# Windowed attention and a four-expert attention layer on one core: zero products, output buffers and a new list of steps

## The chip, the core and the metric

The kernel runs on one core of a Trainium2 chip. The core has five engines with queues of their own: TensorE (PE; its weight loads are PEld), VectorE (DVE), ScalarE (ACT), GpSimd (POOL) and SyncE (SP), which here only issues DMAs. ACT can issue DMAs too. The metric is the device time of one execution in microseconds, lower is better.

## The reference, cut to what matters

```python
# q, k, v: (8 batches, 8 heads, 576 positions, 64), float32
scores = q @ k^T / 8;  keep |i - j| <= 32;  x = softmax(scores) @ v      # (8, 8, 576, 64)
x = x transposed to (8, 576, 512)
w = weights of the 2 largest of 4 gate logits x @ w_gate, softmax over the two
for e in range(4):                                                       # experts, head size 64
    a = causal softmax((x @ wq[e]) @ (x @ wk[e])^T / 8)
    out += w_e * ((a @ (x @ wv[e])) @ wo[e])                             # (8, 576, 512)
```

## The kernel before

All of it is unrolled. A string, `ORDER`, lists some 900 steps, and a loop at the end of the kernel calls one small function for each; so the list sets the order on every engine's queue, and each queue is worked off in order. A step's name is its function and its indices: the first digit is the batch, the next ones the head group, the half or the pair; what stands behind `:` is the engine or the kind of load (`a` ACT, `v` DVE, `g` POOL; `e` a load on SP's queue, `f` one on ACT's), and behind `@` stand the PSUM banks. PSUM has 8 banks; a step that writes a bank waits until the reader of its last content is done.

First half, for a batch `b` and a group `g` of four heads. `lq`, `lk` load q and k (576 KB; the last digit 1 or 2 marks a half of 288 KB) into three rotating buffers each, `qn0` to `qn2` and `kn0` to `kn2` (`NAT`, chosen by (2b+g) mod 3). `tq`, `tk` turn them on DVE into `Tqn`, `Tkn`. `sc` makes the scores of one half of the positions, 80 small products on PE; `ex` takes their exponential on ACT; `mk` multiplies by the window mask on POOL or DVE. `lv` loads v, `vc` copies parts of it to other rows; `av` is the product with v, `un` divides by the sum (DVE). `xt`, `xf`, `xb` transpose the result and bring it to `XTB`.

Second half. `ga`, `gt`, `ge`, `gm`, `gu` make the gate weights. `pp`, `pe` make the experts' q and k, `pv`, `ve` their v; `ps` the scores, `xe` the exponential (ACT), `se` the causal part (POOL), `po` the product with v, `oe` the scaling (DVE), `pt`, `ot` or `dt` the transposed result, `py` the output product. `ye` copies an output part `w` (0, 1: 256 rows; 2: 64 rows) from PSUM to an SBUF tile that `ysb(b, w)` names, and `st` stores it. Before the change the tile is one of three, `Y0` to `Y2`, with 3b+w counted modulo 3, so part `w` always uses `Yw` and has to wait for its store of the batch before. The same three tiles stage the experts' weights at the start (`lw`, then casts `cw`).

`zz` is four products of 128x512 zeros whose result nobody reads. `s_ones`, `s_zero`, `s_pads` clear tiles on DVE. A load is given one more dependence in code: it follows the last PE instruction that stands ahead of it in the list,

```python
        if last_pe[0] is not None:
            tc.add_manual_dep(r.ins, last_pe[0].ins.name, ...
```

so the place of a load among the PE steps sets its earliest issue, and loads that stand ahead of every PE step start at once.

Of the kernel before, what the change touches and what calls it, by code (L numbers as in the profile page):

```python
# [24 lines left out]
NOE = 4  # L25

ORDER = """
    s_ones lq000:e s_ident s_zero lk000:e zz1@3 lq100:e lq011:f lk012:e lk100:e tq000:e tk000:e zz3@6 lk011:f zz2@6
# [4 lines left out]
    av00@0 un03@4 cw11:a un00@0 xt01@6 lq200:e mk1000:v lv10 xf01:a@6 av01@2 mk1001:g un01@2 lk200:e av04@6 xb01:g
    vc10:a un04@6 mk1011:v xt00@4 xf00:a@4 cw10:a xt02@1 sc110@62 cw01:a ex1100@6 lw3 ex1101@2 xb00:g xf02:v@1 xb02:g
    sc111@04 mk1010:g lv14 mk1101:g pp010@6 lwg lv22 lk210:e tq200:e ex1111@4 vc11:g ex1110@0 lq210:e pe010:a@6
    tk200:e pp001@4 pe001:v@4 cw00:a mk1111:v pp011@2 pe011:a@2 pp000@6 mk1110:v pe000:a@6 sc200@40 av12@2 ex2001@0
    ps012@6 lw2 ex2000@4 un12@2 xe012@6 mk1100:g ps000@0 mk2000:g xe000@0 lv23 av10@4 av11@6 ps03@0 cw3:g ps002@2
    xe03@0 un10@4 se012 un11@6 ps011@4 xe002@2 tq210:e av14@1 xt10@6 lk300:e xe011@4 av13@2 mk2001:g cw2:g se000 lv21
    ps001@4 xe001@4 ga0@0 un13@2 lv20 un14@1 xf10:a@6 xt11@2 xf11:a@2 xt12@1 sc201@64 xb10:g xb11:g lq300:e tk210:e
    lv24 xf12:a@1 ex2011@4 pv00@2 lq400:e xb12:g gt0@0 ex2010@6 ga1@1 ge0@0 vc21:a sc210@46 ve00:a@2 lq310:e tk300:e  # L40
    gt1@1 pp101@2 ge1@1 gm0@0 ex2100@4 gm1@1 gu0@0 mk2011:g gu1@1 vc20:g ex2101@6 lk400:e pe101:a@2 mk2010:g pp100@4
    pe100:a@4 sc211@26 pp111@0 ex2110@2 ps100@2 lk310:e tq300:e lv33 mk2101:g ps101@4 mk2100:g ex2111@6 av21@6
    pe111:v@0 pv11@1 mk2110:g xe100@2 xe101@4 un21@6 ve11:a@1 se001 mk2111:g se011 av20@2 pv01@4 av22@0 ve01:a@4
    av23@4 un20@2 un22@0 lv34 ps102@2 ps010@6 lv30 un23@4 se002 av24@1 un24@1 xt21@4 pp110@0 xe102@2 xe010@6 xf21:a@4
    sc300@26 pe110:v@0 lv42 ex3001@6 ex3000@2 sc301@40 xb21:g xt20@6 ex3010@4 se03 xt22@2 se010 se102 xf20:a@6 tk310:e
    tq310:e lv32 lv31 pv10@4 mk3010:g lv41 po00@6 ex3011@0 xf22:v@2 mk3011:v se101 ve10:a@4 ps13@0 ps111@2 po01@4
    se100 xe13@0 xe111@2 mk3001:g oe00@6 ps110@0 sc311@62 xb20:g xb22:g lk500:e xe110@0 oe01@4 sc310@40 ex3110@6
    lq410:e pp201@6 ex3111@2 lv43 lk410:e tk400:e se13 ex3101@0 tq400:e mk3000:v vc31:g ex3100@4 pp200@0 mk3101:g
    pe201:a@6 pe200:a@0 pp210@2 ps200@4 ps112@6 pp211@0 se110 pe210:v@2 vc30:g mk3100:g xe200@4 sc401@24 xe112@6
    pe211:a@0 ex4010@2 tq410:e po10@6 oe10@6 mk3110:g se112 ex4011@4 lv40 ps210@0 av31@2 mk3111:g ps201@4 xe210@0  # L50
    un31@2 tk410:e vc40:g sc400@60 xe201@4 ex4000@6 ps212@4 xe212@4 ex4001@0 av33@2 av32@6 ps211@4 un33@2 ps23@0
    av34@2 ga2@3 xe211@4 pt01@5 xe23@0 un32@6 lq500:e un34@2 pt00@6 ot00:a@6 se111 pt10@2 ot01:v@5 xt31@4 se23 lq510:e
    ot10:a@2 gt2@3 sc411@60 se200 ge2@3 xf31:a@4 xb31:g se201 se212 pv21@2 av30@4 ex4111@0 mk4011:v ve21:a@2 lq600:e
    gm2@3 ex4110@6 lv44 gu2@3 sc410@20 un30@4 vc41:a mk4000:g tq500:e xt30@4 tk500:e mk4111:g pv20@6 ex4100@2 lv50
    xt32@3 ex4101@0 xf30:a@4 py01@0 xf32:a@3 lk510:e xb30:g ve20:a@6 se210 ps202@2 ye01:v@0 xb32:a po11@4 mk4101:g
    pp301@6 mk4010:g xe202@2 sc500@20 oe11@4 pe301:a@6 sc501@64 ex5000@2 ex5001@0 lk600:e pp310@2 tq510:e mk4110:g
    ex5010@6 pp300@6 py02@0 ex5011@4 av43@4 mk4100:g tk510:e lv54 pe310:v@2 pe300:a@6 lv53 un43@4 mk4001:g lv63 av40@6
    pv31@1 ye02:a@0 ps300@2 lv52 un40@6 ve31:a@1 xe300@2 av41@0 un41@0 av42@4 lv61 ps301@2 ps302@6 ga3@1 se211 xe302@6
    un42@4 gt3@1 lv51 xe301@2 ge3@1 se202 av44@0 lv62 un44@0 mk5011:g gm3@1 xt41@6 gu3@1 py00@2 xf41:a@6 pt11@5 xt42@4
    xb41:g xt40@6 mk5001:g ye00:a@2 tk600:e xf42:a@4 po20@0 se302 se301 pp311@2 xf40:a@6 ot11:a@5 pe311:a@2 oe20@0  # L60
    lq610:e xb40:g pv30@4 ve30:v@4 ps311@2 xb42:g sc511@60 xe311@2 ex5111@0 st01 sc510@42 ex5110@6 mk5000:g lk610:e
    ex5100@4 po21@0 mk5010:g lv60 ga4@6 ps33@4 ex5101@2 vc51:g ps312@2 tq600:e vc50:a xe312@2 oe21@0 xe33@4 mk5100:g
    pv40@0 gt4@6 ge4@6 lk700:e tq610:e py11@2 gm4@6 pt20@7 se300 pp401@4 ve40:a@0 pp410@0 ot20:v@7 ye11:a@2 gu4@6
    vc60:g sc600@26 pe401:a@4 ex6000@2 pe410:v@0 sc601@04 tk610:e mk5110:g ex6010@0 mk5111:g mk5101:g se311 se33
    tk700:e lq700:e pp400@2 po30@0 vc61:g ex6001@6 pe400:a@2 pp411@6 ex6011@4 av51@4 oe30@0 lv64 un51@4 pe411:a@6
    av50@2 av53@0 pv41@6 ve41:a@6 av52@4 ps43@6 un50@2 un53@0 un52@4 ps310@2 ps401@0 xe43@6 av54@6 xt50@4 mk6011:g
    pt21@7 xe310@2 xe401@0 un54@6 sc611@20 ot21:v@7 tq700:e xf50:a@4 sc610@46 ex6110@2 ex6111@0 ps400@2 xt51@0 se312
    ex6100@4 ex6101@6 xe400@2 xb50:g mk6110:v xt52@4 mk6111:v st00 se310 mk6010:v st02 xf52:v@4 py10@6 av62@2 xf51:a@0
    un62@2 se401 py12@5 ye10:a@6 av63@0 ye12:a@5 se43 un63@0 ps402@4 lq710:e ps411@2 xb52:a mk6101:v xe402@4 mk6100:v
    xe411@2 xb51:g pp511@6 se402 pe511:a@6 pp500@0 sc700@42 pe500:a@0 mk6001:v sc701@60 ex7000@4 lv70 ex7001@2 ps410@4  # L70
    ex7010@6 mk7001:g xe410@4 st12 mk6000:v ex7011@0 po31@2 st11 pp501@6 pp510@4 pe501:a@6 av60@6 tq710:e lk710:e
    oe31@2 pe510:v@4 ps53@0 xe53@0 un60@6 st10 lv71 ps502@4 ps501@2 pv51@0 se400 py22@1 xe502@4 dt31 ve51:v@0 xe501@2
    lv73 av61@6 ye22:v@1 dt30 un61@6 ps412@4 py21@0 lv72 xe412@4 po40@6 ye21:v@0 ps500@2 st21 oe40@6 ps512@0 tk710:e
    ga5@5 av64@4 xe512@0 xt61@0 gt5@5 se412 lv74 xe500@2 un64@4 xt60@6 xf61:a@0 py20@2 se411 ye20:a@2 ge5@5 pv50@0
    xf60:v@6 se410 gm5@5 mk7000:g xt62@2 xf62:a@2 xb60:g xb62:a py31@6 ve50:a@0 ye31:a@6 vc71:a po41@2 xb61:g se501
    gu5@5 oe41@2 mk7011:g pp611@4 se502 se500 pp600@0 pe600:v@0 pe611:a@4 pp601@6 pe601:v@6 se53 sc710@02 sc711@64
    ex7100@0 ex7101@2 ex7111@4 mk7100:v po50@0 vc70:g mk7101:g pp610@4 ex7110@6 st20 ps601@6 mk7110:g oe50@0 py30@2
    pe610:v@4 ps602@0 ye30:v@2 xe601@6 mk7010:g ps612@6 dt41 av70@4 xe602@0 st22 av71@2 ps511@0 mk7111:v xe612@6
    un70@4 ps610@6 un71@2 xe511@0 av74@4 xe610@6 un74@4 se602 st31 ga6@5 ps600@2 ps611@0 xe600@2 av73@6 py32@4 xe611@0
    gt6@5 ye32:a@4 un73@6 av72@2 st30 ps63@0 xe63@0 xt70@6 xt72@4 ge6@5 ps510@0 un72@2 xf72:v@4 xt71@2 xf70:a@6 dt40  # L80
    st32 xe510@0 se511 dt50 py41@6 pv60@0 xb72:g se611 se601 xb70:g gm6@5 xf71:a@2 se512 se610 py42@3 ye41:v@6
    ve60:a@0 ye42:v@3 pv61@2 py40@6 gu6@5 se510 se612 ve61:a@2 se600 po51@0 ye40:a@6 xb71:g pp711@2 oe51@0 st42 st41
    pp701@4 se63 pe701:a@4 pp700@0 pe711:v@2 pe700:a@0 dt51 pp710@6 pe710:a@6 po61@2 ps73@4 ps701@6 py51@0 oe61@2 st40
    xe73@4 ps702@4 ps710@2 xe701@6 po60@6 dt61 xe702@4 ye51:a@0 oe60@6 pv70@4 xe710@2 py50@6 se702 ps700@0 ps712@2
    ve70:a@4 xe700@0 dt60 xe712@2 ye50:v@6 ga7@5 pv71@7 gt7@5 py52@4 se700 se73 ye52:v@4 ve71:a@7 ge7@5 se701 gm7@5
    st51 gu7@5 ps711@0 py61@6 st50 po701@4 xe711@0 py60@2 oe701@4 ye61:a@6 st52 se711 se712 st61 ye60:a@2 po711@1
    se710 po700@7 py62@6 pt701@4 st60 oe711@1 oe700@7 ye62:a@6 po710@6 pt711@5 ot701:a@4 ot711:a@5 py711@3 ye711:a@3
# [581 lines left out]
```

## Time and profile before

| | us |
|---|---|
| median of 3 runs (range) | 236.62 (236.04 to 237.95) |
| the profiled execution, whole | 235.26 |
| its span, first to last instruction | 233.5 |
| PE busy in the span | 215.5 |
| mean granted clock of TensorE | 0.971 |

The span is what the trace shows; 1.76 us of the execution lie around it. The profiled execution is 1.36 us shorter than the median.

### The profile page before, as it was taken

To read this page: it belongs to the slowest core of one execution; us is meant where nothing else is said; L and a number is where in the kernel's file an instruction comes from. 1 tells how busy PE (TensorE), PEld (TensorE's weight loads), DVE (VectorE), ACT (ScalarE), POOL (GpSimd) and SP (SyncE) were. 2 spreads that over 40 slices of the span, in tenths; PEclk is the share of its full clock that TensorE was granted. 3 is DMA by queue.
4 is the path that set the end of the run, shared out by engine and by line. 5 is a ranking of instruction groups with operands and counts; after the bars stand their busy time and mean duration, and the time that the engine had idled before them with its cause. 6 is when DMAs were issued, how large, how long until landed. Compare 5 with 4: busy or idle time off the path is not lost.

```text
span 233.5 us, 12313 instructions
## 1 busy us (share of the span) xinstructions
PE 215.5 (92%) x5516; PEld 171.3 (73%) x5516; DVE 179.1 (77%) x366; ACT 156.1 (67%) x232; POOL 137.3 (59%) x173
## 2 busy tenths in 40 slices
...
GB/s 241 409 173 238 167 221 273 239 218 218 298 176 107 146 183 211 11 219 181 186 164 136 253 192 104 140 3 104 158 259 199 177 107 121 55 140 121 225 215 201
DMA packets 60518, 41.97 MB, mean 180 GB/s; under 512 B 50736, under 2 KB 51760, under 8 KB 60464
## 3 DMA queue, kind: packets, MB, share of 16 engines
...
q10 hardware_dynamic: 432, 0.85, 1.0%
...
## 4 chain that ended last, share of the span: by engine, by line
PE 65%; DVE 9%; ACT 2%; issue 2%; DMA 2%; SPq 0%; ACTq 0%; DVEq 0%
PE PS L178 58%; PE PS L181 7%; DVE A L342 2%; DVE Tkn L293 2%; DVE Tqn L293 2%; DMA out_dram<-Y 2%; DVE Y L172 1%; DVE QKE L172 1%; ACT V L170 1%; ACT VE L170 0%; DVE OE L571 0%; ACT A L338 0%; DVE XN L370 0%; ACT OTT L170 0%; ACT AT L511 0%
## 5 line engine op out<-in xcount | busy, mean ns | idle before, releaser
L342 POOL TENSOR_TENSOR A<-A,MASKP 128x576 f32<-128x576 f32 x48 | 68.0, 1432 | 15.3 <-ACT A L338 15.2
L515 ACT ACTIVATE ATE<-PS 128x1024 bf16<-128x1024 f32 x48 | 47.6, 1022 | 14.4 <-PE PS L178 14.2
L338 ACT ACTIVATE A<-PS 128x576 f32<-128x576 f32 x64 | 38.4, 651 | 21.8 <-PE PS L178 21.6
L178 PE MATMUL PS<-Tqn,Tkn 32*64 32x128 f32 (+3 forms) x2560 | 46.5, 283 | 6.4 <-DVE Tkn L293 2.6
L178 PEld LDWEIGHTS PS<-Tqn,Tkn 32*64 32x64 f32 x2560 | 41.6, 139 | 13.0 <-DVE Tkn L293 3.5
L172 POOL CAST XTB<-XTF 128x1024 bf16<-128x1024 f32 (+1 forms) x26 | 19.4, 770 | 40.7 <-ACT XTF L170 31.6
L293 DVE STREAM_TRANSPOSE Tqn<-qn 128x576 f32<-128x576 f32 (+1 forms) x34 | 37.2, 1177 | 5.4 <-DMA qn<-in_q_dram 5.4
L178 PE MATMUL PS<-V,A 128*64 128x65 f32 (+1 forms) x1280 | 39.9, 223 | 1.2 <-DVE A L342 0.7
L178 PEld LDWEIGHTS PS<-V,A 128*64 128x64 f32 (+1 forms) x1280 | 36.2, 132 | 5.7 <-issue 1.7
L518 POOL TENSOR_SCALAR_AFFINE_SELECT ATE<-ATE 128x256 bf16<-128x256 bf16 x64 | 25.5, 420 | 22.5 <-ACT ATE L515 15.0
L293 DVE STREAM_TRANSPOSE Tkn<-kn 128x576 f32<-128x576 f32 (+1 forms) x34 | 37.0, 1177 | 0.2 <-DMA kn<-in_k_dram 0.2
L370 DVE TENSOR_TENSOR XN<-PS,RC 128x512 f32<-128x512 f32 x32 | 22.1, 692 | 1.1
L178 PE MATMUL PS<-WO,OTT 128*128 128x512 bf16 (+1 forms) x96 | 20.1, 346 | 0.5 <-ACT OTT L170 0.3
L181 PE MATMUL PS<-ident,XN 128*128 128x128 f32 x144 | 19.3, 278 | 0.1
L170 ACT COPY XTF<-PS 128x1024 f32<-128x1024 f32 (+1 forms) x23 | 16.8, 761 | 3.5 <-PE PS L181 3.2
L178 PEld LDWEIGHTS <-ATE 128*128 128x128 bf16 x448 | 15.9, 97 | 3.7 <-issue 2.0
L178 PE MATMUL PS<-WV,XTB 128*128 128x256 bf16 (+1 forms) x192 | 18.5, 255 | 0.1
L178 PE MATMUL PS<-XTB,WK 128*128 128x288 bf16 x128 | 18.0, 286 | 0.2 <-ACT VE L170 0.2
L178 PE MATMUL PS<-VE,ATE 128*128 128x65 bf16 x448 | 17.1, 193 | 1.0 <-ACT Y L170 1.0
L170 ACT CAST QKE<-PS 128x576 bf16<-128x576 f32 x21 | 13.4, 643 | 6.7 <-PE PS L178 6.6
L178 PE MATMUL PS<-XTB,WQ 128*128 128x288 bf16 x128 | 17.8, 286 | 0.0
L178 PE MATMUL PS<-QKE 64*128 64x64 bf16 (+4 forms) x192 | 17.0, 278 | 0.1
...
## 6 DMA issues: line engine op xcount, KB each, us to landing
qn<-in_q_dram SPq DMA_DIRECT2D x15, 576.0 KB, 4.8
kn<-in_k_dram SPq DMA_DIRECT2D x15, 576.0 KB, 4.8
...
```

Source lines behind the costliest of these rows:

```text
L170: nc.scalar.copy(o, i)
L172: eng(c).tensor_copy(o, i)
L178: last_pe[0] = nc.tensor.matmul(*a, **kw)
L181: last_pe[0] = nc.tensor.transpose(*a)
L293: nc.vector.transpose(T[:, :].rearrange("q (p o) -> q o p", o=18)[:, o0:o1], n_[:, o0:o1, 32 * dh:32 * dh + 32])
L338: nc.scalar.activation(AT[(2 * b + g) % NAT_][half][p], two(b0)[:, :, 0:HS], EXP, scale=scale_att)
L342: eng(c).tensor_tensor(out=ap, in0=ap, in1=MASK[:, None, HS * half:HS * half + HS].to_broadcast([128, 2, HS]), op=MULT)
L370: nc.vector.tensor_tensor(out=XN[T // 2][:, T % 2, :].rearrange("p (g h d) -> p g h d", g=2, h=4), in0=u[:, :, :, 0:64], in1=rc[:, :, :, N ...
L515: nc.scalar.activation(chunk(ATE[(2 * b + j) % len(ATE)], ch), two(b0), EXP, scale=scale_moe)
L518: nc.gpsimd.affine_select(ap, ap, pattern=[[0, n], [1, w]], compare_op=IS_GE, fill=0.0, base=0, channel_multiplier=-1)
```

## The change

It has three parts. There are seven `zz` steps in place of five (28 zero products in place of 20): four ahead of the first scores in place of three, none between the first four `sc`, two behind them, and one behind `sc200`. `ysb` gives other tiles to the last two batches: parts 1 and 2 of batch 6 go to `qn1` and `kn1`, part 0 of batch 7 to `Y1`, its parts 1 and 2 to `qn2` and `kn2`, all at a time when the q and k in them are no longer in use. And `ORDER` is a new list. Its length, 908 steps against 906, is that of the old one and the two `zz`; which engine does a copy differs in places.

```diff
 ORDER = """
-    s_ones lq000:e s_ident s_zero lk000:e zz1@3 lq100:e lq011:f lk012:e lk100:e tq000:e tk000:e zz3@6 lk011:f zz2@6
-    s_pads lq110:e sc001@60 tq011:e lq012:e tk011:e ex0011@0 ex0010@6 lv01 tk012:e lv03 s_warm tq012:e s_mask sc000@40
...
+    lq000:e lk012:e s_ones s_zero s_pads tq000:e lk000:e lk011:f zz2@0 s_ident lq011:f tk000:e lq100:e tq011:e zz1@3
+    tk012:e lq012:e tk011:e lw10 lq110:e zz5@5 s_mask zz3@1 sc001@06 ex0011@6 ex0010@0 lk100:e tq012:e lv02 mk0010:g
+    mk0011:g sc000@26 ex0000@2 tq100:e lk110:e ex0001@6 sc010@42 ex0100@4 lv00 tk100:e lv03 ex0101@2 lv01 cw10:g
+    sc011@04 mk0100:v s_warm zz4@2 tq110:e zz6@2 ex0111@4 mk0000:g lw11 lv04 lw01 sc100@62 ex0110@0 ex1000@6 mk0111:g
...
+    ps73@2 se701 py52@0 gm7@1 xe73@2 se73 ps710@2 xe712@4 se712 xe710@2 ye52:a@0 gu7@1 po701@6 se710 dt60 py61@4
+    po711@2 py60@0 ye61:a@4 po700@4 oe701@6 py62@5 ye60:a@0 oe711@2 oe700@4 pt701@7 po710@3 st51 pt711@2 ot701:a@7
...
     def ysb(b, w):
-        return YSB[(3 * b + w) % len(YSB)]
+        if b < B - 2 or (b == B - 2 and w == 0):
+            return YSB[(3 * b + w) % len(YSB)]
+        if b == B - 1 and w == 0:
+            return YSB[1]
+        g = (2 * b) % NNAT if b == B - 1 else (2 * b + 1) % NNAT
+        t = NAT["qn" if w == 1 else "kn"][g]
+        return t[:, 0:16, :].rearrange("p o d -> p (o d)").rearrange("p (a n) -> p a n", n=DM)
```

The start of SP's queue before. The names are the buffers of q, k and v; `kn_65` is `kn0`, `kn_66` is `kn1`, 576 columns are a half.

```order
L184 DMA qn_62<-in_q_dram 128x1152
L184 DMA kn_65<-in_k_dram 128x1152
L184 DMA qn_64<-in_q_dram 128x1152
L184 DMA kn_66<-in_k_dram 128x576
L184 DMA kn_67<-in_k_dram 128x1152
L184 DMA qn_62<-in_q_dram 128x1152
L184 DMA qn_63<-in_q_dram 128x576
L184 DMA V_76<-in_v_dram 128x8x64 x3
```

And now:

```order
L184 DMA qn_62<-in_q_dram 128x1152
L184 DMA kn_66<-in_k_dram 128x576
L184 DMA kn_65<-in_k_dram 128x1152
L184 DMA qn_64<-in_q_dram 128x1152
L184 DMA qn_63<-in_q_dram 128x576
L184 DMA Y_113<-in_moe_wk_dram 128x8x64
L184 DMA qn_62<-in_q_dram 128x1152
L184 DMA kn_67<-in_k_dram 128x1152
L184 DMA V_76<-in_v_dram 128x8x64
```

A half of the second group's k now stands ahead of the first group's k. On ACT's queue the other half of it (`lk011:f`) has changed places with a half of q (`lq011:f`), and stands ahead of every PE step. The second q half and a weight load came forward, a whole k went back.

The start of DVE's queue, as the difference. `XTF` to `WG` are the tiles that `s_pads` clears, `Tqn_68` to `Tkn_73` the first group's transposes.

```order
 L211 MEMSET ZERO 128x256
-L293 STREAM_TRANSPOSE Tqn_68<-qn_62 128x18x32
-L293 STREAM_TRANSPOSE Tqn_69<-qn_62 128x18x32
-L293 STREAM_TRANSPOSE Tkn_72<-kn_65 128x18x32
-L293 STREAM_TRANSPOSE Tkn_73<-kn_65 128x18x32
 L223 MEMSET XTF_93 128x4x32
 L224 MEMSET XTF_93 128x4x32
```

The four transposes of the first group stood ahead of the clearing of tiles, and now stand behind it.

The end of ACT's queue before, from the last exponential on, with the buffers' numbers; `OTT1` is the transposed result of batch 7.

```order
L515 ACTIVATE ATE0_101<-PS_61 128x1024
L170 COPY Y1_113<-PS_61 128x1024
L170 COPY Y0_112<-PS_61 128x1024
L170 COPY Y2_114<-PS_61 128x256
L170 COPY OTT1_111<-PS_61 128x320 x2
L170 COPY Y1_113<-PS_61 128x512 x2
L170 COPY Y0_112<-PS_61 128x512
```

And now:

```order
L515 ACTIVATE ATE0_101<-PS_61 128x1024 x2
L170 COPY Y2_114<-PS_61 128x256
L170 COPY qn1_63<-PS_61 128x1024
L170 COPY Y0_112<-PS_61 128x1024
L170 COPY OTT1_111<-PS_61 128x320 x2
L170 COPY kn1_66<-PS_61 128x256
L170 COPY qn2_64<-PS_61 128x512 x2
L170 COPY Y1_113<-PS_61 128x512
```

Six different tiles take the output copies there, and the copy of batch 5's last part stands at the head of them, which was on DVE and earlier before; the two copies to `OTT1` still stand behind the big ones.

## Rows read from the trace of the kernel before

**Rows 1.** The page: busy time of each engine, share of the span, instructions.

```profile
PE 215.5 (92%) x5516; PEld 171.3 (73%) x5516; DVE 179.1 (77%) x366; ACT 156.1 (67%) x232; POOL 137.3 (59%) x173
```

**Rows 2.** Busy time by stretch; behind the engines the granted clock, DMA share, GB/s.

```profile
4.90:8.30 3.40, 1.28 (x21) 0.52 (x19) 3.40 (x4) 1.28 (x1) 0.63 (x3) 1.00 1.02 409
8.30:15.10 6.80, 5.82 (x161) 4.54 (x148) 5.80 (x26) 2.33 (x5) 1.62 (x2) 0.50 0.87 295
15.10:22.00 6.90, 4.45 (x177) 2.98 (x176) 6.60 (x8) 2.65 (x5) 6.90 (x6) 0.99 0.85 219
22.00:25.40 3.40, 3.40 (x139) 3.39 (x134) 3.30 (x4) 2.45 (x3) 3.40 (x3) 0.50 0.98 218
...
31.00:60.00 29.00, 27.32 (x791) 22.46 (x790) 24.32 (x44) 22.71 (x33) 21.20 (x22) 1.00 0.88 237
60.00:215.00 155.00, 153.24 (x3965) 125.17 (x3964) 123.27 (x247) 112.65 (x170) 95.10 (x120) 1.00 0.57 154
215.00:228.40 13.40, 11.95 (x162) 6.89 (x159) 8.44 (x29) 9.97 (x16) 2.64 (x7) 1.00 0.63 210
```

**Rows 3.** Timeline of the start: start us, us, what, count, idle before it.

```profile
1.48 4.43 PE L178 MATMUL PS<-ZERO 128*128 128x512 bf16 x12 [1.48 <-DVE ZERO L211]
...
4.55 2.34 DVE L293 STREAM_TRANSPOSE Tqn<-qn 128x576 f32<-128x576 f32 x2 [3.13 <-DMA qn<-in_q_dram]
...
6.73 2.32 DVE L293 STREAM_TRANSPOSE Tkn<-kn 128x576 f32<-128x576 f32 x2
...
8.03 0.56 PE L178 MATMUL PS<-Tqn,Tkn 32*64 32x64 f32 x16 [2.12 <-DVE Tkn L293]
9.01 0.17 DVE L223 MEMSET XTF<- 128x128 f32 x1
...
9.11 2.29 PE L178 MATMUL PS<-Tqn,Tkn 32*64 32x64 f32 x68 [0.52 <-DVE Tkn L293]
...
11.13 1.20 DVE L293 STREAM_TRANSPOSE Tqn<-qn 128x288 f32<-128x288 f32 x2
...
15.40 1.26 DVE L293 STREAM_TRANSPOSE Tqn<-qn 128x288 f32<-128x288 f32 x2 [0.92 <-DMA qn<-in_q_dram]
...
16.18 2.85 PE L178 MATMUL PS<-Tqn,Tkn 32*64 32x64 f32 x160 [0.55 <-DVE Tqn L293]
...
20.87 1.02 PE L178 MATMUL PS<-ZERO 128*128 128x512 bf16 x4 [1.84 <-ACT A L338]
...
26.64 0.55 PE L178 MATMUL PS<-Tqn,Tkn 32*64 32x96 f32 x21 [1.02 <-issue]
...
27.12 3.02 PE L178 MATMUL PS<-V,A 128*64 128x65 f32 x96
...
34.57 2.51 PE L178 MATMUL PS<-Tqn,Tkn 32*64 32x96 f32 x160
```

**Rows 4.** The first load of k: its issue in the timeline.

```profile
1.27 0.42 SPq L184 DMA_DIRECT2D kn<-in_k_dram  x1
```

**Rows 5.** The same load in the DMA view: size, us from issue to landing.

```profile
kn<-in_k_dram SPq DMA_DIRECT2D x1, 576.0 KB, 4.8
```

**Rows 6.** Busy time of one stretch of the start, columns as in rows 2.

```profile
6.00:7.00 1.00, 0.00 (x0) 0.00 (x0) 1.00 (x2) 0.73 (x1) 0.00 (x0) 1.00 1.01 412
```

**Rows 7.** The page: the exponentials of the window scores (count, busy, mean ns, idle).

```profile
L338 ACT ACTIVATE A<-PS 128x576 f32<-128x576 f32 x64 | 38.4, 651 | 21.8 <-PE PS L178 21.6
```

**Rows 8.** Timeline of the end, as in rows 3.

```profile
222.36 1.01 ACT L170 COPY Y<-PS 128x1024 f32<-128x1024 f32 x1 [0.52 <-DMA out_dram<-Y]
...
224.27 0.37 ACT L170 COPY Y<-PS 128x256 f32<-128x256 f32 x1 [0.90 <-DMA out_dram<-Y]
...
224.69 0.34 PE L178 MATMUL PS<-VE,ATE 128*128 128x65 bf16 x6 [0.98 <-ACT Y L170]
...
228.46 0.69 DVE L172 COPY Y<-PS 128x512 f32<-128x512 f32 x1 [0.59 <-PE PS L178]
228.55 1.12 SPq L618 DMA_DIRECT2D out_dram<-Y  x2
...
229.77 0.53 SPq L622 DMA_DIRECT2D out_dram<-Y  x1
```

More of the change, by code (lines that the diff above doesn't have):

```diff
@@ L33 @@
[L33 to L87, printed above, removed]
@@ new lines @@
+    sc011@04 mk0100:v s_warm zz4@2 tq110:e zz6@2 ex0111@4 mk0000:g lw11 lv04 lw01 sc100@62 ex0110@0 ex1000@6 mk0111:g
+    mk0110:g tk110:e ex1001@2 vc01:g sc101@62 mk0001:v vc00:a ex1010@6 lk200:e lv10 av02@0 mk0101:v lv13 av03@6 un02@0
+    mk1010:g un03@6 av00@4 un00@4 ex1011@2 xt01@2 cw11:g lq200:e xf01:a@2 av04@7 un04@7 lw00 av01@0 xt02@7 un01@0
+    mk1011:g xt00@4 mk1000:g xf02:a@7 lv14 cw01:g tk200:e tq200:e xb02:a xb01:g mk1001:v lv12 sc110@02 xf00:a@4 lv11
+    xb00:g sc111@46 ex1100@0 ex1101@2 pp001@0 lwg cw00:a ex1110@4 vc10:g ex1111@6 pp000@2 lk210:e mk1111:v lw2
```

57 lines of the change are left out of this document (52 added, 5 removed).

## The prediction, made before the changed kernel ran

> **What bounds the kernel now.** I read the page's busy times first: PE is busy for 215.5 of 233.5 us, no other engine for more than 179.1 [rows 1]. Such a share is an average, so the table by stretch came next. From 60 to 215 us PE is busy for 153.24 of 155 us, from 31 to 60 for 27.32 of 29 [rows 2]: there the kernel is its PE work, and a new order can win back at most the idle 1.76 and 1.68 us. The remaining idle time and all of the slow clock lie at the two ends. Up to 31 us PE waits for loads, for the transposes on DVE and for banks, and the granted clock is 0.50 (1.2 GHz instead of 2.4) from 8.3 to 15.1 and from 22.0 to 25.4 us [rows 2]; a group of 160 score products takes 2.51 us at full clock, so 80 take 1.25, while 68 took 2.29 at the low level, so 80 take 2.7 [rows 3]. The end, from 215 on, has 1.45 us of idle PE [rows 2] and then some 5 us of last copy, store and landing. The timeline of both ends shows what each wait was for [rows 3, 8]; there the new list is followed step by step.
>
> **The start, step by step.** Landmark: the first product with v, step `av02`, starts at 27.12 us [rows 3]; what comes behind it is nearly solid PE work, so whatever the start gains or loses arrives at the end.
>
> Loads. The first k was issued at 1.27 us and took 4.8 us to land [rows 4, 5], so it was there at 6.07. In this stretch the DMA engines are full, share 1.01 at 412 GB/s [rows 6], so a half load (0.295 MB) costs 0.72 us of them. Now one half stands ahead of this k on SP's queue and another is issued at once from ACT's: 1.44 us, and the q half that follows on ACT's queue takes up to 0.72 more. So k lands between 7.5 and 8.2 us; I take 8.1, since the q half is issued before k's data would be through. The Trainium skill ("DMA: Bandwidth & Descriptors", section "Issuing engines are not separate DMA queues") says that DMAs run on the same 16 engines and interleave whichever engine issued them, which speaks against a gain from the second queue; the full share above agrees with it, and were it false k would land at 6.8.
>
> DVE. Two transposes of k take 2.32 us [rows 3]: the first is done at 9.3, both at 10.4. PE's first real product starts at 9.3 instead of 8.03. But then DVE is ahead: the clearing of pads, which stood from 9.01 to 11.13 in the middle of the transposes, now fits into the 3.13 us in which DVE waited for the first q, and the 0.92 us wait for the last q half goes, since that load no longer stands behind `sc001` [rows 3]. Four pairs of half transposes at 1.2 us [rows 3] end at 15.2, instead of 16.66, for which PE had idled 0.55 us in front of 16.18 [rows 3]. Two whole pairs at 2.33 bring batch 1's first group to 19.9.
>
> PE, with the low clock as in the trace. `sc001` waits until 10.4 for the second transpose and needs 2.0 us for its other 64 products: 12.4. `sc000` needs a bank that an exponential frees (0.65 us [rows 7]) and 2.7 us of work, with some overlap as in before: 15.2. `sc010` needs another bank: 0.65, then 2.7, to 18.6. `sc011` the same: 21.9. Then eight zero products, and here the clock decides. Before, it came back at 15.1, after 5.82 busy us of 6.80, and at 25.4, after 3.40 of 3.40 [rows 2]. I take it as back at 22: the zeros then take 0.22 us each, to 23.6, `sc100` ends at 24.9, two exponentials free the banks of `sc101` at 26.2, it ends at 27.4, and the copy of v behind them on ACT lets `av02` go at 27.7: **0.6 us later** than before. The 1.02 us "issue" wait of before [rows 3] needs two score groups back to back, and is gone, since the exponentials now part them; this is in the sum already. Bounds: 2.5 us earlier and 2.8 later, worked out under the rivals.
>
> **The other parts.**
> - The zero products of the start lie where PE waits anyway. The seventh set, behind `sc200`, stands in the solid stretch. Four cost 0.86 us at full clock (1.02 [rows 3] less the last one's overlap); uncovered it is all paid, covered it is nothing, since PE idles 1.68 us between 31 and 60. I take 0.4.
> - 31 to 60: `av04` got a bank of its own, `av12`, which waited for masks, stands later, and the zeros stand in part of the rest. Of the 1.68 us I take 0.7 as won, between 0 and 1.4.
> - 60 to 215: the new list has about as many places as the old at which a result is needed at once: -0.3, within -1.3 and +1.3. No engine gets a new load near PE's: the moved copies are a few us of 179.1 at most [rows 1].
> - The end. Two output copies on ACT waited 0.52 and 0.90 us for an earlier store to finish reading `Y0` and `Y2`, and the second held PE for 0.98 [rows 8]. With tiles of their own neither waits; the small copy could start when its product is there, some 0.75 us earlier. What is late next is ACT itself: the two copies to `OTT1` stand behind a 1.01 us copy, as before, and the output product needs both. Following the list from `ps702`, I find PE idle for 0.3 us (bank of `py52`), 0.6 (`po711`, behind the last exponentials and their causal part) and 0.75 (`py710`, behind the two `OTT1` copies): 1.65, against 1.45 now. Counting each step's own time to the last product gives 0.55 less than before. Between 0.2 and -0.55 I take -0.3. The last store is no nearer: before it waited from 229.15 (228.46 + 0.69) to 229.77 for SP to issue two small stores [rows 8]; in the new list these again stand right ahead of it. That wait stays, or grows by 0.2.
>
> Sum: 0.6 + 0.4 - 0.7 - 0.3 - 0.3 = -0.3. The profiled execution, 235.26 (span 233.5 and 1.76 around it), becomes 234.96; the median of the runs lies 1.36 above it, so the forecast as a median is **236.3 us**, with -2.2 and +2.4 from the smaller bounds added up in part: 234.3 to 238.7.
>
> **Rivals.**
>
> *The clock stays up (faster).* The low stretch from 8.3 came after PE had idled from 5.91 to 8.03, the one from 22.0 after it idled for 1.84 us before 20.87 [rows 2, 3]. Four more zero products before the scores, run at full clock, carry PE to 6.6, and the eight later ones fill the place of the second gap. If that is enough: `sc001` ends at 11.5, `sc000` at 13.4, `sc010` waits for DVE's 15.2 and ends at 16.5, `sc011` at 18.4, zeros to 20.1, `sc100` to 21.4, `sc101` to 23.9; the copies of v let `av02` go at 24.6, so -2.5 instead of +0.6. With the seventh set covered and the end at its better bound: 236.3 - 3.1 - 0.4 - 0.25 = 232.5. Against it: 9.3 is still 2.7 us behind the last zero, and the waits for banks and for 15.2 leave further gaps. The Trainium skill ("TensorE: Matmul & The Clock Gate", "Part 1: The HAM clock gate") has this rule: the throttled state is the default and activity releases it. The trace agrees as to the sign; it does not show that so few zeros do.
>
> *The first k is late and the clock stays low until 25.4 (slower).* If the waits for k and for banks keep the clock at 0.50 until the zeros have run, these take twice 0.22 us each, 3.5 in all, to 25.9 with bank waits of the full 0.65; `sc100` ends at 27.1, `sc101` at 29.7, `av02` goes at 29.9: +2.8. The seventh set uncovered, 0.86, and an end of +0.35, with 0.7 won in between: 236.62 + 3.3 = 239.9. It decides if k lands after some 7.5 us and the clock is still low at 22. For it: the share of 1.01. Against it: 3.3 us of PE idle between 31 and 215 could take up some of it.
>
> *The buffers do nothing* is in the forecast: the end gains 0.3.
>
> **How the numbers follow.** The forecast has a chance of 0.42, the first rival 0.36 (also with other ways for the list to be better, as the middle at its good bound), the second 0.22. Within 1%, about what a measurement of this kernel can tell from no change, lies 234.3 to 239.0; so faster 0.36, same 0.42, slower 0.22. The range leaves out a tenth beyond each outer case: 232.0 to 239.7.
>
> **What would show it.** In the profile of after: the first `Tkn` transpose at about 8.1; the first score product at 9.3; the granted clock between 8.3 and 25; `av02`'s start against 27.12; no wait of `Y` or `qn` copies for a store; PE's last product some 18 us behind the last `pp`. The forecast is wrong if the clock follows another pattern, or if the solid stretch from 31 to 215, which I read as equal, has waits of more than 5 us or next to none.

## The result, and the profile after

The changed kernel takes 239.02 us (median of 20 runs, 236.19 to 244.43), the kernel before, on the same chip, 235.52 (20 runs, 233.6 to 238.38). The ratio is 1.0121, with an interval of 1.0088 to 1.0153: slower by 1.2%, about 2.9 us, where the forecast was no change. The medians are of all runs, while each ratio compares only those runs of the two kernels that lie within 1.5% of their kernel's fastest, so the quotient of the medians can differ from it. The profiled execution took 242.55 us (span 240.8), longer than the median, and part of that is a clock that fell in mid-kernel; further profiles of the same kernel, below, stand beside it where a size matters.

The page and the table by stretch of the changed kernel answer to [rows 1] and [rows 2]; the columns are the same.

```profile
PE 219.5 (91%) x5509; PEld 173.8 (72%) x5524; DVE 183.5 (76%) x367; ACT 152.2 (63%) x232; POOL 139.9 (58%) x172
```

```profile
8.30:15.10 6.80, 4.32 (x207) 3.55 (x208) 6.80 (x11) 2.39 (x4) 2.31 (x2) 1.00 1.04 320
15.10:22.00 6.90, 4.92 (x126) 3.61 (x117) 5.99 (x7) 2.48 (x5) 3.04 (x5) 0.60 0.78 209
22.00:25.40 3.40, 3.07 (x85) 1.69 (x83) 3.40 (x4) 0.31 (x1) 3.34 (x3) 0.82 0.35 71
...
31.00:60.00 29.00, 26.96 (x743) 21.79 (x745) 22.96 (x40) 17.21 (x29) 20.35 (x19) 1.00 0.83 210
60.00:215.00 155.00, 150.59 (x3923) 123.89 (x3916) 121.84 (x242) 111.29 (x168) 99.61 (x121) 0.98 0.54 150
```

Two things stand out. From 60 to 215 us TensorE is idle for 4.41 us, not 1.76, and its granted clock is no longer 1.00: the largest difference is in the stretch that the prediction called solid. And VectorE is busy for 183.5 us instead of 179.1, though it runs 367 instructions instead of 366. The start, for all its new order, ends where it was forecast. Its timeline in the changed kernel answers to [rows 3]:

```profile
1.47 5.93 PE L178 MATMUL PS<-ZERO 128*128 128x512 bf16 x16 [1.47 <-DVE ZERO L211]
...
7.79 2.34 DVE L293 STREAM_TRANSPOSE Tkn<-kn 128x576 f32<-128x576 f32 x2
...
9.11 0.48 PE L178 MATMUL PS<-Tqn,Tkn 32*64 32x64 f32 x16 [1.70 <-DVE Tkn L293]
...
10.19 1.33 PE L178 MATMUL PS<-Tqn,Tkn 32*64 32x64 f32 x68 [0.60 <-DVE Tkn L293]
...
12.15 1.37 PE L178 MATMUL PS<-Tqn,Tkn 32*64 32x96 f32 x76 [0.63 <-ACT A L338]
...
21.36 2.39 PE L178 MATMUL PS<-ZERO 128*128 128x512 bf16 x6 [0.22 <-issue]
...
27.59 1.10 PE L178 MATMUL PS<-V,A 128*64 128x65 f32 x26
```

The first score product starts at 9.11 us (forecast 9.3) and the first product with v at 27.59 (forecast 27.7).

So what happened between 60 and 215? The waits of TensorE in that stretch have one large entry, 3.4 us for the tile `OE` that VectorE writes at line 571. Followed back, VectorE was late with it because one mask, step `mk3001`, took 4.68 us. First VectorE around it, then GpSimd (POOL) and TensorE in the same stretch, then the table by stretch:

```profile
77.87 4.68 DVE L342 TENSOR_TENSOR A<-A,MASKP 128x576 f32<-128x576 f32 x1
82.47 2.33 DVE L293 STREAM_TRANSPOSE Tqn<-qn 128x576 f32<-128x576 f32 x2
...
85.11 0.82 DVE L571 TENSOR_TENSOR OE<-PS,RG 128x640 bf16<-128x640 f32 x1
```

```profile
77.13 1.47 POOL L172 COPY V<-V 64x1536 f32<-64x1536 f32 x1
78.57 1.40 POOL L342 TENSOR_TENSOR A<-A,MASKP 128x576 f32<-128x576 f32 x1
79.92 2.01 POOL L172 CAST XTB<-XTF 128x1024 bf16<-128x1024 f32 x2
```

```profile
82.23 0.39 PE L178 MATMUL PS<-QKE 64*128 64x448 bf16 x4
85.99 4.27 PE L178 MATMUL PS<-Tqn,Tkn 32*64 32x64 f32 x160 [3.37 <-DVE OE L571]
```

```profile
82.50:84.70 2.20, 0.12 (x4) 0.00 (x0) 2.20 (x4) 1.02 (x1) 0.88 (x3) 1.00 0.44 101
84.70:91.50 6.80, 5.51 (x166) 4.95 (x167) 4.54 (x9) 1.85 (x4) 3.19 (x2) 0.50 0.06 11
```

A mask on VectorE takes 0.75 us when nothing is beside it (four of them took 2.74 us in the kernel `port` below). This one began at 77.87, while GpSimd was in a copy, and ended at 82.55, which is 0.62 us behind the end of GpSimd's last cast (79.92 + 2.01 = 81.93). All the while GpSimd went from one instruction into the next without a pause. Then TensorE ran dry for 3.37 us, up to 85.99, and from 84.70 on its granted clock was at 0.50, the lower of its two levels, for 6.8 us. In the kernel before, `mk3001` stood on GpSimd; the new list has it as `mk3001:v`.

At the end of the program, the copies to the new tiles no longer wait for a store, as they did in [rows 8]. But the last store is issued later behind its copy than before (0.62 us there). VectorE's last copy and SP's last issues in the changed kernel:

```profile
234.87 0.69 DVE L172 COPY Y<-PS 128x512 f32<-128x512 f32 x1 [0.60 <-PE PS L178]
```

```profile
235.40 1.49 SPq L624 DMA_DIRECT2D out_dram<-kn  x2
236.99 0.52 SPq L628 DMA_DIRECT2D out_dram<-Y  x1
```

The copy is done at 235.56, its store is issued at 236.99: 1.43 us.

### The profile page after: what moved, and what is told of

The parts are those of the page before. It is cut to its first block, busy times and chain, and to the rows that moved or that the text cites. A ratio compares the mean times of both kernels' runs of the same rounds, so it can differ in the third digit from the quotient of the medians.

```text
span 240.8 us, 12288 instructions
## 1 busy us (share of the span) xinstructions
PE 219.5 (91%) x5509; PEld 173.8 (72%) x5524; DVE 183.5 (76%) x367; ACT 152.2 (63%) x232; POOL 139.9 (58%) x172
## 4 chain that ended last, share of the span: by engine, by line
PE 75%; DMA 8%; DVE 7%; issue 5%; ACT 2%; SPq 0%; DVEq 0%; ACTq 0%
PE PS L178 68%; PE PS L181 7%; DMA qn<-in_q_dram 3%; DVE Tkn L293 3%; DMA kn<-in_k_dram 3%; DMA Y<-in_moe_wq_dram 2%; DVE Tqn L293 2%; DVE OE L571 1%; ACT A L338 1%; SPq L184 0%; ACT ATE L515 0%; ACT OTT L170 0%; DVE XN L370 0%; DVE Y L172 0%; ACT WQ L170 0%
## 5 line engine op out<-in xcount | busy, mean ns | idle before, releaser
L342 POOL TENSOR_TENSOR A<-A,MASKP 128x576 f32<-128x576 f32 x47 | 66.3, 1425 | 24.4 <-ACT A L338 24.2
L515 ACT ACTIVATE ATE<-PS 128x1024 bf16<-128x1024 f32 x48 | 48.3, 1027 | 15.4 <-PE PS L178 13.9
L518 POOL TENSOR_SCALAR_AFFINE_SELECT ATE<-ATE 128x256 bf16<-128x256 bf16 x64 | 24.7, 405 | 35.1 <-ACT ATE L515 31.2
L172 POOL COPY V<-V 64x2048 f32<-64x2048 f32 (+1 forms) x14 | 24.4, 1745 | 11.8 <-DMA V<-in_v_dram 7.2
L172 POOL CAST XTB<-XTF 128x1024 bf16<-128x1024 f32 (+1 forms) x20 | 16.3, 833 | 16.2 <-ACT XTF L170 16.1
L170 ACT COPY XTF<-PS 128x1024 f32<-128x1024 f32 (+1 forms) x22 | 15.9, 750 | 10.1 <-PE PS L181 10.0
L342 DVE TENSOR_TENSOR A<-A,MASKP 128x576 f32<-128x576 f32 x17 | 20.2, 1204 | 1.6 <-ACT A L338 1.6
L178 PE MATMUL PS<-WO,OTT 128*128 128x512 bf16 (+1 forms) x83 | 18.5, 342 | 1.5 <-ACT OTT L170 0.7
L170 ACT COPY Y<-PS 128x1024 f32<-128x1024 f32 (+2 forms) x17 | 14.2, 845 | 5.8 <-PE PS L178 5.2
L178 PE MATMUL PS<-QKE 64*128 64x64 bf16 (+4 forms) x192 | 17.7, 278 | 0.1
```

Source lines behind the costliest of these rows:

```text
L170: nc.scalar.copy(o, i)
L172: eng(c).tensor_copy(o, i)
L178: last_pe[0] = nc.tensor.matmul(*a, **kw)
L342: eng(c).tensor_tensor(out=ap, in0=ap, in1=MASK[:, None, HS * half:HS * half + HS].to_broadcast([128, 2, HS]), op=MULT)
L515: nc.scalar.activation(chunk(ATE[(2 * b + j) % len(ATE)], ch), two(b0), EXP, scale=scale_moe)
L518: nc.gpsimd.affine_select(ap, ap, pattern=[[0, n], [1, w]], compare_op=IS_GE, fill=0.0, base=0, channel_multiplier=-1)
```

## The experiments

Theory P, from the profile: the new list puts a mask on VectorE beside a stretch in which GpSimd works without pause; the mask is held back by GpSimd, what is queued behind it on VectorE comes late, TensorE waits and its clock falls. Rivals: the start (loads and clock) differs between executions and makes the difference; the new tiles themselves cost something; the new list is longer for TensorE as a whole; the end has become longer.

**The changed kernel once more**, with nothing changed.

> The changed kernel once more, nothing edited, for a second profile. Theory P (a mask on DVE, mk3001, waits while POOL works without a pause): the profile again has one DVE mask of some 4.7 us near 78 us, where others take 0.75, and PE idle for 3 us or more behind it; time about 1.012 of the kernel before. Theory S (the start: first k 1.7 us later, clock low until 23 us): the long mask was an accident of the first profiled execution and is not there; the loss of about 3 us is all in the first 31 us, with the first product with v at 29 to 30.

241.23 us (6 runs, 238.15 to 303.35), ratio 1.0156, interval 1.0090 to 1.0222. The loss stands. Its profile, however, does not show what P expected: the mask took 2.01 us there, not 4.7, and TensorE had no wait for VectorE behind it.

```profile
91.26 2.01 DVE L342 TENSOR_TENSOR A<-A,MASKP 128x576 f32<-128x576 f32 x1
```

That execution is the one of 303.35 us, with a granted clock of 0.65 on average, so its times can't be set beside the others; that the long wait does not come every time can be read from it.

**One word: the mask on GpSimd again.**

```
-    pv10@4 ex3011@0 mk3001:v xb22:a po00@6 ...
+    pv10@4 ex3011@0 mk3001:g xb22:a po00@6 ...
```

> The changed kernel with one mask, mk3001, put on POOL instead of DVE, at the same place of the list. Theory P: the 4.7 us instruction on DVE and the 3.4 us of idle PE behind it go, POOL gets 1.4 us more; 2 to 3 us faster than the changed kernel, so 1.000 to 1.004 of the kernel before. Theory S: the wait moves or was not there, and the time stays at 1.012, within 0.4%.

236.58 us (12 runs), ratio 1.0003, interval 0.9961 to 1.0046. The loss goes with this one word, as far as the interval tells. In its profile TensorE has no wait for VectorE between 60 and 100 us, and the clock stays at 1.00 from 21.6 us to 236.7.

**The new list with the old result tiles, and the old list with the new ones.** The edits exchange the function `ysb` alone.

> The new list with the three old output tiles for all batches. If the new tiles are worth what the trace of before showed, 0.5 to 1.0 us at the end, this is 0.2 to 0.4% slower than the changed kernel, 1.014 to 1.017 of before. If ACT's chain at the end takes their place, as the prediction had it, there is no difference (1.010 to 1.014). Neither theory on the loss has a part in it.

> The old list with the new output tiles for the last two batches, nothing else. The two waits of ACT for a store, 0.52 and 0.90 us, go, and with them up to 0.98 us of idle PE; the output copy that is late next is the pair to OTT1. Expected 0.3 to 1.0 us faster than before, 0.996 to 0.999.

The first: 241.81 us (6 runs), ratio 1.0240, interval 1.0177 to 1.0303. In the new list a copy of batch 6 stands before the store of batch 5 that reads the same tile `Y`, so with the old tiles part of the result is overwritten before it is stored; the list needs the new tiles, and this time, longer than was expected, says only that without them the copies wait longer for stores (behind 210 us ACT waits 3.5 us for one store, and TensorE 2.5 us for the copy behind it). The second: 235.09 us (12 runs), ratio 0.9946, interval 0.9910 to 0.9983. The tiles alone are a gain of 1.3 us; the loss is the list's.

**Three masks of the old list moved from VectorE to GpSimd**, with the new tiles and without. In the trace of the kernel before three masks on VectorE are drawn out as well, to 1.87, 1.93 and 1.97 us. The first of these, and GpSimd beside it:

```profile
86.24 1.87 DVE L342 TENSOR_TENSOR A<-A,MASKP 128x576 f32<-128x576 f32 x1
```

```profile
86.03 1.46 POOL L172 COPY V<-V 64x1536 f32<-64x1536 f32 x1
87.46 3.30 POOL L342 TENSOR_TENSOR A<-A,MASKP 128x576 f32<-128x576 f32 x2
```

The copy ends at 87.49 and VectorE's mask at 88.11, 0.62 us later. The edit:

```
-    ... mk1110:v ... mk3011:v ... mk3000:v ...
+    ... mk1110:g ... mk3011:g ... mk3000:g ...
```

> The list of before with the new result tiles (235.09, ratio 0.9946), and three masks that took 1.87 to 1.97 us on VectorE (mk1110, mk3011, mk3000; 0.75 when alone) moved to GpSimd, where one takes 1.41. Theory P (a mask on VectorE waits while GpSimd works, and what stands behind it on VectorE is late): VectorE gets 5.7 us back and TensorE's three waits behind them (0.73, 0.72, 0.55 in the trace of before) go, so 233.0 to 234.5, ratio 0.985 to 0.993. Rival Q (those waits are only the first of several that end at nearly the same time, ACT's copies being next): within 0.5 us of 235.1. Rival R (GpSimd, with 4.2 us more in stretches where it has no pause, brings its own casts late): 236 or more.

> The kernel before with the three masks mk1110, mk3011 and mk3000 on GpSimd and nothing else changed. If the gain of the version with new result tiles as well (233.78, ratio 0.9893) is the sum of the tiles' (0.9946) and the masks', this gives 0.994 to 0.996: 234.2 to 234.8. Rival: the two need each other (the end or the middle hides the other's gain): within 0.2 per cent of before, or all of the gain, 0.990.

With the new tiles: 233.78 us (12 runs), ratio 0.9893, interval 0.9842 to 0.9943. With the old ones: 235.05 us (12 runs), ratio 0.9978, interval 0.9940 to 1.0015. The first is within what P expected and is faster than both kernels of this case. The second alone is not told from no change, and the first is not told from the tiles' 0.9946 (the intervals overlap); 0.9978 times 0.9946 is 0.9924, inside the interval of the first, so nothing speaks against a plain sum. TensorE's waits from 31 to 215 us, by releaser (sum, times, longest), in the old list with the new tiles:

```profile
PE PS L178 <- DVE QKE L172: 1.4, 2, 0.7
PE PS L178 <- issue: 1.3, 3, 0.7
PE PS L178 <- DVE OE L571: 0.6, 1, 0.6
PE PS L178 <- DVE A L342: 0.5, 1, 0.5
```

and with the three masks on GpSimd as well:

```profile
PE PS L178 <- issue: 0.7, 1, 0.7
PE PS L178 <- DVE QKE L172: 0.4, 1, 0.4
```

The waits for `OE` and for a mask are gone, and one of the two for `QKE`: three things that stood behind a drawn-out mask on VectorE. In the two other profiles with these three masks on GpSimd (`b_masks_pool`, `b_best_st72`) TensorE still waits 0.8 and 0.6 us for `OE`; only the wait for a mask is in none of the three.

**The same move the other way**, in the old list with the new tiles: `mk3001:g` becomes `mk3001:v`.

> The list of before with the new result tiles, and one word changed in the other direction: mask mk3001 on VectorE in place of GpSimd, as the changed kernel has it. Theory P: the mask is drawn out beside GpSimd's casts that stand right behind it (2 us or more for 0.75), two of VectorE's masks are then drawn out within 9 us, and TensorE waits 1 to 3 us more: 236 to 238. Rival (the 4.68 us stall belongs to the new list's order alone, since GpSimd is freed of 1.41 us here): no change from 235.1, within 0.6.

235.89 us (12 runs), ratio 0.9988, interval 0.9951 to 1.0024, against 0.9946 without the move. TensorE now waits 1.1 us for a mask of VectorE and 0.9 for `OE`; the mask took 1.54 us. The sign is P's, but the mask was to take 2 us or more, the size (0.8 us) lies below P's range, and the intervals overlap: this alone decides nothing. A mask on VectorE costs much only in some places.

**GpSimd's neighbours taken away instead.** In the changed kernel, `mk3001` stays on VectorE; the casts `xb20`, `xb21` and the copy `vc30` go to ACT.

> The changed kernel with mask mk3001 left on VectorE, but the GpSimd work around it taken to ACT: casts xb20 and xb21 and the copy vc30. Theory P: with GpSimd holding only the mask mk3010 near it, mk3001 takes at most 2.2 us in the profile and the loss of 2 to 3 us is partly given back; ACT gains some 3 us of work there, so 236.5 to 238.5. Rival (mk3001 is long for a reason of its own, such as the exponentials it reads, or VectorE's order): it still takes 2 to 4.7 us and the time stays at 239 to 241.

239.04 us (6 runs), ratio 1.0133, interval 1.0074 to 1.0191. The mask took 1.95 us, as P had it, but nothing came back, and the time is the rival's: ACT's 3.5 us more stand in the same stretch, and TensorE now waits 1.0 us for `ATE` and 0.5 for `VE`, both ACT's. The test is inconclusive, since the cure costs as much as the disease, and since the mask takes 1.95 to 2.01 us in some executions of the changed kernel too, as above and below.

**More masks on GpSimd in the new list**: `mk3001` and also `mk1100`, `mk2011` and `mk6110`.

> The changed kernel with four masks moved from VectorE to GpSimd: mk3001 as before, and mk1100, mk2011 and mk6110, which took 1.3 to 1.7 us there. With mk3001 alone the time was 236.58, ratio 1.0003. Theory P: VectorE gets some 2 us more back in the stretches 31 to 60 and 150 to 180, but TensorE has no wait on a mask left there in that trace (its waits are issue, WQ and XN), so 235.5 to 236.6. If masks were costly wherever they stand, 234 to 235. Rival (GpSimd late): 237 or more.

239.47 us (12 runs), ratio 1.0091, interval 1.0039 to 1.0142: slower than with `mk3001` alone, which was the rival here. TensorE's two longest waits from 31 to 215 us show why:

```profile
PE PS L178 <- POOL A L342: 1.8, 1, 1.8
PE PS L178 <- POOL XTB L172: 1.6, 1, 1.6
```

Here GpSimd is the one that is late, with a mask and with a cast behind it. Where both engines are full, a mask moved is a wait moved.

**The seventh set of zero products taken out**, with `mk3001` on GpSimd.

```
-    ... sc200@46 zz0@2 lv23 ...
+    ... sc200@46 lv23 ...
```

> The changed kernel with mk3001 on GpSimd (236.58, ratio 1.0003) and without the seventh set of zero products behind the scores of batch 2. The set lasts about 0.9 us on TensorE. If TensorE is the bound there, 0.4 to 0.9 us come back: 235.7 to 236.2. Rival: it fills a wait, so nothing changes, or TensorE's clock falls somewhere between 31 and 60 us for want of work and the time rises to 237 or more.

236.98 us (12 runs), ratio 1.0018, interval 0.9976 to 1.0060, against 1.0003: no gain that can be measured. The rival that the zeros fill a wait fits best.

**The wait by itself.** Two kernels hold nothing but masks on VectorE beside rows of GpSimd.

> The disputed cost by itself; nothing of the reference is computed, the result is filled with ones. VectorE runs four masks (two inputs in SBUF, 128x576) alone; then four beside eight masks of GpSimd that wait for nothing; four beside ten casts 128x1024; four beside eight copies 64x1536; then four casts from PSUM (one input) beside eight masks; then the three rows of GpSimd alone. Theory P: alone 0.75 us each; beside GpSimd each waits at least to the end of the running instruction (1.4, 1.0, 1.47), and where GpSimd has no pause it may be passed over several times, as the 4.68 us row says: 1.5 to 6 us each; casts from PSUM stay at 0.75. Rival (a mask gets in at each boundary of GpSimd's instructions, so the wait never exceeds one of them and the 4.68 us had another part): four masks take turns with GpSimd's, at most 2.2 us each, and GpSimd's own grow by about 0.6 each.

> The disputed wait by itself again; nothing of the reference is computed, the result is filled with ones. GpSimd repeats the row of the changed kernel (copy 64x1536, mask, three casts) with no wait between; VectorE runs 0 to 6 short copies from PSUM (0.28 us each) and then one mask, so that the mask arrives at seven points of the first two instructions of GpSimd; each twice. If the point of arrival decides, the masks that arrive in some part of an instruction (the last fifth, say) are passed over and take more than 2.1 us; if nothing but the running instruction counts, each takes what is left of that instruction and 0.6 us more, never over 2.1.

In the first, VectorE's rows are: four masks alone; beside GpSimd's masks; beside its casts; beside its copies; then four one-input casts from PSUM beside its masks.

```profile
17.77 2.74 DVE L67 TENSOR_TENSOR A<-A,MASKP 128x576 f32<-128x576 f32 x4
...
21.06 7.54 DVE L67 TENSOR_TENSOR A<-A,MASKP 128x576 f32<-128x576 f32 x4
...
34.46 6.01 DVE L67 TENSOR_TENSOR A<-A,MASKP 128x576 f32<-128x576 f32 x4
...
46.81 7.70 DVE L67 TENSOR_TENSOR A<-A,MASKP 128x576 f32<-128x576 f32 x4
...
60.62 2.74 DVE L91 CAST QKE<-PS 128x576 bf16<-128x576 f32 x4
```

and GpSimd's eight masks, beside VectorE's four and later beside the casts from PSUM:

```profile
20.98 12.94 POOL L67 TENSOR_TENSOR AG<-AG,MASKP 128x576 f32<-128x576 f32 x8
...
60.47 10.89 POOL L67 TENSOR_TENSOR AG<-AG,MASKP 128x576 f32<-128x576 f32 x8
```

So the two engines take turns: four masks take 7.54 us instead of 2.74, each waiting for one GpSimd instruction and no more, and GpSimd pays 2.05 us for the four. A cast that reads PSUM is not touched. In the second kernel a mask that arrives 0.17 to 1.16 us into a copy of 1.46 takes 1.97 to 0.91 us, each time what is left of the copy and 0.6 more. Here P is right that masks wait, and wrong that a row without pause passes them over: none of the masks beside GpSimd (12 in the first kernel, 14 in the second) waits for more than the running instruction, whether it arrives 0.07 to 0.59 us into a mask, a cast or a copy (first kernel) or 0.17 to 1.36 us into a copy (second). The 4.68 us do not follow from this.

**How often is the long wait?** Three more profiles of the changed kernel.

> The changed kernel as it is, one profiled execution. If the long wait is what it usually pays, mask mk3001 takes 3 us or more, TensorE waits some 3 us about 82 to 86 us and the granted clock falls after it. If it was an accident, the mask takes 1.4 to 2.2 us, TensorE waits under 1.5 us there and its clock stays.

> As for the first look: 3 us or more for mk3001 if the long wait is usual, 1.4 to 2.2 us if not.

> As for the first look: 3 us or more for mk3001 if the long wait is usual, 1.4 to 2.2 us if not.

Their times were 241.15, 240.69 and 238.79 us. `mk3001` and GpSimd beside it in the first:

```profile
77.40 4.67 DVE L342 TENSOR_TENSOR A<-A,MASKP 128x576 f32<-128x576 f32 x1
```

```profile
76.66 1.47 POOL L172 COPY V<-V 64x1536 f32<-64x1536 f32 x1
78.10 1.40 POOL L342 TENSOR_TENSOR A<-A,MASKP 128x576 f32<-128x576 f32 x1
79.45 2.01 POOL L172 CAST XTB<-XTF 128x1024 bf16<-128x1024 f32 x2
```

and in the second (the third is alike, with 1.95 us):

```profile
79.81 1.96 DVE L342 TENSOR_TENSOR A<-A,MASKP 128x576 f32<-128x576 f32 x1
```

```profile
77.41 1.46 POOL L172 COPY V<-V 64x1536 f32<-64x1536 f32 x1
79.74 1.41 POOL L342 TENSOR_TENSOR A<-A,MASKP 128x576 f32<-128x576 f32 x1 [0.87 <-ACT A L338]
81.55 1.11 POOL L172 CAST XTB<-XTF 128x1024 bf16<-128x1024 f32 x1 [0.40 <-ACT XTF L170]
```

The long wait is neither an accident nor the rule: with `a_again` it came in two of five profiles of the changed kernel, to 0.01 us the same. It came where VectorE's mask began 0.74 us into GpSimd's copy, and GpSimd went from the copy through its mask into the two casts without a pause. In the second and the third GpSimd itself waited for the exponentials, 0.87 and 0.42 us, VectorE's mask began 0.07 us behind GpSimd's, and it was let in after that one instruction. The kernel with the old result tiles (`a_old_buffers`) has the same list and stands between:

```profile
80.25 2.20 DVE L342 TENSOR_TENSOR A<-A,MASKP 128x576 f32<-128x576 f32 x1
```

```profile
78.99 1.47 POOL L172 COPY V<-V 64x1536 f32<-64x1536 f32 x1
80.43 1.41 POOL L342 TENSOR_TENSOR A<-A,MASKP 128x576 f32<-128x576 f32 x1
82.00 2.34 POOL L172 CAST XTB<-XTF 128x1024 bf16<-128x1024 f32 x2 [0.16 <-ACT XTF L170]
```

VectorE's mask began within the copy, GpSimd's mask passed it over, and it was let in behind that one, where GpSimd waited 0.16 us for ACT. So in all six traces it was let in at the first point at which GpSimd had to wait. This is no general rule: in the kernel before, the mask at 86.24 was let in between a copy and a mask of GpSimd that had no pause between them, as in `port`.

In both profiles with the long wait TensorE then waited 3.4 us for `OE` and its clock fell to 0.50, for 6.8 and 3.4 us; in the second and the third of the new ones it waited 0.6 us there and the clock stayed. What this costs is read between the same two exponentials of ACT, which stand at 65.03 and 96.89 us in the first profile of the changed kernel: 31.9 and 30.9 us with the long wait, 28.5 and 28.7 with the short one. With the mask on GpSimd and the rest of this stretch unchanged it is 27.8, 28.4 and 28.3 (`a_mk3001_pool`, `a_mk3001_st72`, `a_mk3001_no_zz`). The long wait therefore costs 2.5 to 4.1 us, and the short one is not told from none. In two of five executions that makes 1.0 to 1.6 us on average, less than the 2.4 to 2.8 us that the one word gave in time. Nor is it known how often the runs behind the ratios have the long wait: the two executions that show it took 242.55 and 241.15 us, both above the median of 239.02, and so did one with the short wait (240.69).

**The last store.** With `mk3001` on GpSimd the last store is issued even 1.93 us behind its copy, since two small stores (`st72`) stand ahead of it on SP's queue. They go to ACT's queue, behind its last store; the same in the fastest version.

```
-    ... st711 st72 py701 ye701:a st701:t ...
+    ... st711 py701 ye701:a st701:t st72:t ...
```

> The changed kernel with mask mk3001 on GpSimd (236.58, ratio 1.0003), and the two small stores that stand ahead of the last store on SP's queue (st72) issued from ACT's queue behind its last store. If the SP queue sets the end, the last big store is issued some 0.2 us after its copy in place of 1.9, and 1.0 to 1.7 us come off: 234.9 to 235.6, ratio 0.993 to 0.996. Rival: the small stores then land last themselves, issued by ACT about 1 us after its store, or the landing is limited by the transfers: within 0.5 us of 236.6.

> The same move in the old list with the new tiles and three masks on GpSimd (233.78, ratio 0.9893), where SP issues the last store 0.18 us after its copy already. Theory: 0 to 0.3 us, 233.5 to 233.8; if the small stores now land last, 0.5 us longer. A gain of 1 us would say that something other than SP's queue is moved.

236.98 us (12 runs), ratio 1.0029, interval 0.9983 to 1.0074, and 233.80 us (12 runs), ratio 0.9931, interval 0.9889 to 0.9972. No gain in either. The store was now issued 0.03 us behind its copy (the copy, begun at 233.47, ends at 234.16):

```profile
233.47 0.69 DVE L172 COPY Y<-PS 128x512 f32<-128x512 f32 x1 [0.59 <-PE PS L178]
```

```profile
234.05 1.77 ACTq L624 DMA_DIRECT2D out_dram<-kn  x2
```

```profile
234.19 0.33 SPq L628 DMA_DIRECT2D out_dram<-Y  x1
```

but ACT needed until 235.82 to issue the small stores, and the last big ones took 3.4 to 4.1 us to land. (With the small stores ahead of it, in `a_mk3001_pool`, the last one on SP's queue took 2.2 us to land, and here 4.1.) The order on SP's queue is not what sets the end; this theory fell.

## Why the prediction was wrong

**The start: right in size, in part by luck.** The first k was there at 7.77 us (forecast 8.1, between 7.5 and 8.2, and 6.8 had the second queue been a gain), the first score product came at 9.11 (9.3) and `av02` at 27.59 (27.7). The clock took another way to the same place: 1.00 from 6.2 to 16.4, then 0.50 to 23.2. So the first two groups of scores ended at 11.52 and 13.52 us, as the faster rival had it (11.5 and 13.4), and what that won was lost again behind 16.4. In the three later profiles `av02` starts at 26.23, 28.30 and 26.02, so a term of +0.6 is within what executions differ by, and neither rival's price (-2.5, +2.8) was paid.

**The seventh set of zeros, +0.4:** taking it out changed 1.0003 to 1.0018, so the lower bound of 0 is nearer.

**31 to 60, -0.7:** not seen. TensorE's idle time is 2.04 us instead of 1.68.

**60 to 215, -0.3: this is the step that failed.** It rested on the sentence that no engine gets a new load near TensorE's, the moved copies being a few us of VectorE's 179.1. The load is indeed small (VectorE gains 4.4 us in all, 3.9 of them the waiting of one mask). What the step left out is that a mask's duration depends on what GpSimd does beside it, so that one word in a list moves not 0.75 us but 2.0 or 4.7, and that behind it on VectorE stands work that TensorE needs at once. (The list changes the engine of 23 of the 64 masks, 12 of them to VectorE and 11 from it; the account of the change does not name this.) The runs put it at this: the word `mk3001:v` is worth 1.0121 against 1.0003, about 2.8 of the 2.9 us that were lost by the ratio, and 2.4 us between the medians. This one word alone, at +2.4 to +2.8, lies beyond the step's bound of +1.3. The profile of before had the evidence: masks of 1.87 to 1.97 us on VectorE where others took 0.75, and waits of TensorE of up to 0.7 us behind them; the prediction counted places where results are needed at once and did not ask why equal instructions differ. Its last paragraph names the failure: the stretch which I read as equal has waits.

The mechanism, as far as it is shown: a mask (two inputs in SBUF) and GpSimd's work exclude one another, instruction by instruction; the kernel with nothing else in it shows this, and that a one-input read of PSUM is free of it. The Trainium skill ("SBUF — State Buffer", section "SBUF: two separate sides") states it as an exclusive lock on a port pair that the two engines share, taken for a whole instruction by whoever starts first, by a VectorE operation with two SBUF inputs among others; the trace agrees (0.75 us alone, 1.95 beside a mask of 1.40). That the word costs time is shown by the run that changes it back; the way from the drawn-out mask over TensorE's wait to the lower clock is shown in two executions, and if two in five is the rule it makes up about half of the time. Open is what makes up the rest, and why the mask was let in only after four GpSimd instructions in two of five profiles, when by itself, and elsewhere in these kernels, it is let in after one. The end, 0.62 us behind GpSimd's last cast, says that GpSimd held it, not who chose.

**The end, -0.3:** in the changed list nothing was won. From TensorE's last product of kind `pp` to the end of the span it is 23.1 us before and 23.1 after. The tiles alone, in the old list, bring this to 21.9, which is their gain of 1.3 us; the new list gives it back. Its last store waits 1.43 us for SP instead of the forecast's 0.62 to 0.82, but the last experiment shows that this wait is covered by something else. The landing of the many late stores (3.4 to 4.1 us with the small stores moved, against 2.1 to 2.7 in the old list with the same edit) is the likely cover; this is argued, not shown.

With `mk3001` on GpSimd the new list still stands 0.6% behind the old one with the same tiles (1.0003 against 0.9946, which is at the edge of the noise). Zeros and SP's queue were tried and are not it. The end is most of it if the 23.1 and 21.9, from one profile each, hold in general. Another candidate is not tested: from 31 to 215 us TensorE has 2.4 to 3.8 us of waits that the profile puts down to issue, in the three profiles of the new list with this mask alone on GpSimd, and 0.2 to 1.3 in the four of the old list with the new tiles.
